# Sparse attention and a maxout layer on one core: a hand-set order up to the first maxout, v one batch ahead

## The chip, the cores and the metric

One core of one Trainium2 chip. The metric is the device time of one execution in microseconds (us), as a median over runs. The kernel before takes 225.36 us (three runs, 224.71 to 225.65). The profile's span is 1 to 2 us shorter than that time.

Engines are named as in the profile: PE multiplies matrices (PEld loads its weights), DVE and ACT work on vectors, POOL is the third vector engine, SP only issues DMAs. "PEq", "SPq", "POOLq" are the instruction queues of an engine.

## The reference, cut to what matters

```python
# q, k, v: [4 batches, 8 heads, 768 positions, 64], float32
k_sum = k.reshape(B, H, nb, 32, D).max(axis=3)      # 24 blocks per head
v_sum = v.reshape(B, H, nb, 32, D).mean(axis=3)
mask_l = np.abs(pos[:, None] - pos[None, :]) < 16   # a band
# softmax over [band scores, block scores + log 32], times [v, v_sum]
x = attention.transpose(0, 2, 1, 3).reshape(3072, 512)
out = np.maximum(x @ w1, x @ w2) @ w_out            # d_model 512, d_ff 1024
```

Both kernels rewrite the maxout as `x @ (w1 @ w_out) + relu(x @ (w2 - w1)) @ w_out`. The product `w1o = w1 @ w_out` is made once, on the chip, and so is a piece of work with no counterpart in the reference.

## The kernel before

Queries are cut into 12 tiles of 64. A tile needs the 96 positions of k around it and 24 block sums. The same 96 positions of v are gathered by copies from `vb` into `vext`. The block means of v go into `vext` too: a matmul makes them (`vs_ps`), a DVE copy writes tile 0, and one broadcast DMA fills the other 11 tiles. These are the parts that the change touches:

```python
def load_batch(b):                      # all on SP's queue, in this order
    for hp in range(NP):
        for src, tag in ((k, "kf"), (q, "qf"), (v, "vf")):
            loads[tag, b, hp] = load_pair(src, b, hp, tag)

def prep_v(b):
    vbt, vx = vb[b % 2], vext[b % 2]
    for hp in range(NP):
        nc.vector.tensor_copy(...)      # cast of v, four times      (cut)
    for j in range(2):
        r = j * 48
        nc.sync.dma_start(out=vx[r:r + 48, 0], in_=vbt[0:48, 0, j])
        nc.sync.dma_start(out=vx[r:r + 48, 1:NT:4], in_=vbt[24:72, :, j])
        # ... six more for each j: 16 copies in all                  (cut)
    ps = psum.tile([128, H, D], F32, tag="tr", bufs=2, name="vs_ps")
    # ... six matmuls of the means into ps                           (cut)
    nc.vector.tensor_copy(out=vx[96:NK, 0, :, 0:D], in_=ps[96:NK])
    nc.sync.dma_start(...)              # the broadcast              (cut)

load_batch(0)
prep_v(0)
load_weights()
for _ in attention(0):
    pass
cast_weights()
make_w1o()
for b in range(B):
    side = iter(())
    if b + 1 < B:
        load_batch(b + 1)
        prep_v(b + 1)
        side = attention(b + 1)
    for _ in maxout(b):                 # one step of each in turn
        next(side, None)
    for _ in side:
        pass
```

The softmax here doesn't subtract the row's maximum and nothing guards it: scores larger than these inputs give would overflow.

Of the kernel before, what the change touches and what calls it, by code (L numbers as in the profile page):

```python
# [12 lines left out]
F32 = mybir.dt.float32  # L13
# [7 lines left out]
def kernel(  # L21
# [23 lines left out]
    NK = 96 + nb  # L45
    VW = 66

    def g0(t):
        return 0 if t == 0 else (336 if t == NT - 1 else 32 * t - 8)
# [5 lines left out]


    identity = const.tile([128, 128], BF16, name="identity")
    make_identity(nc, identity[:])
# [3 lines left out]
    m0 = const.tile([128, 3, 64], F32, name="m0")  # L62
    m1 = const.tile([128, 3, 64], F32, name="m1")
    for m, j in ((m0, 0), (m1, 1)):
        nc.gpsimd.memset(m[:], 1.0)
        for w, off in enumerate((0, -16, -32)):
            base = off - 95 * j
            sl = m[:, w, :]
            nc.gpsimd.affine_select(out=sl, in_=sl, compare_op=ALU.is_ge, fill=0.0,
                                    base=base + window - 1, channel_multiplier=2,  # L70
                                    pattern=[[-1, 64]])
            nc.gpsimd.affine_select(out=sl, in_=sl, compare_op=ALU.is_ge, fill=0.0,
                                    base=window - 1 - base, channel_multiplier=-2,
                                    pattern=[[1, 64]])
    nc.gpsimd.affine_select(out=m0[:], in_=m0[:], compare_op=ALU.is_ge, fill=0.0,
                            base=47, channel_multiplier=-1, pattern=[[0, 3], [0, 64]])
    nc.gpsimd.affine_select(out=m1[:], in_=m1[:], compare_op=ALU.is_ge, fill=0.0,
                            base=-48, channel_multiplier=1, pattern=[[0, 3], [0, 64]])
    nc.gpsimd.tensor_tensor(out=m0[:], in0=m0[:], in1=m1[:], op=ALU.add)
    nc.gpsimd.memset(m0[96:128], 1.0)  # L80
    mask = const.tile([128, NT, 64], BF16, name="mask")
    nc.gpsimd.tensor_copy(out=mask[:, 0:2, :], in_=m0[:, 0:2, :])
    nc.gpsimd.tensor_copy(out=mask[:, NT - 2:NT, :], in_=m0[:, 1:3, :])
    nc.gpsimd.tensor_copy(out=mask[:, 2:NT - 2, :],
                          in_=m0[:, 1:2, :].to_broadcast([128, NT - 4, 64]))

    bias = const.tile([128, 1], F32, name="bias")
    nc.gpsimd.memset(bias[:], 0.0)
    nc.gpsimd.memset(bias[96:128], logblk)


    amean = const.tile([128, 3, 128], BF16, name="amean")
    nc.gpsimd.memset(amean[:], 1.0 / block)
    nc.gpsimd.affine_select(out=amean[:], in_=amean[:], compare_op=ALU.is_ge, fill=0.0,
                            base=96 * 16, channel_multiplier=1, pattern=[[128, 3], [-16, 128]])
    nc.gpsimd.affine_select(out=amean[:], in_=amean[:], compare_op=ALU.is_ge, fill=0.0,
                            base=15 - 96 * 16, channel_multiplier=-1,
                            pattern=[[-128, 3], [16, 128]])


    NBUF = 3
    kext = [const.tile([128, NT, 128], BF16, name=f"kext{i}") for i in range(NBUF)]
    qbd = [const.tile([128, NT, 128], BF16, name=f"qbd{i}") for i in range(NBUF)]
    NPB = 4
    prob = [const.tile([128, 8 * 128], BF16, name=f"prob{i}") for i in range(NPB)]
    vb = [const.tile([128, 3, 2, H, VW], BF16, name=f"vb{i}") for i in range(2)]
    vext = [const.tile([128, NT, H, VW], BF16, name=f"vext{i}") for i in range(2)]
    for i in range(NBUF):
        nc.gpsimd.memset(qbd[i][0:64, :, 64:128], 0.0)
        nc.gpsimd.memset(qbd[i][64:128, :, 0:64], 0.0)  # L110
        nc.gpsimd.memset(kext[i][:, :, NK:128], 0.0)
    for i in range(NPB):
        nc.vector.memset(prob[i][:], 0.0)
    for i in range(2):
        nc.gpsimd.memset(vb[i][:, :, :, :, D:VW], 1.0)
        nc.gpsimd.memset(vext[i][96:NK, :, :, D:VW], 1.0)

# [3 lines left out]
    w1b = const.tile([128, KC, d_ff], BF16, name="w1b")  # L121
    w1t = const.tile([128, FC, d_model], BF16, name="w1t")
# [14 lines left out]
    def load_batch(b):  # L137
        for hp in range(NP):
            for src, tag in ((k, "kf"), (q, "qf"), (v, "vf")):
                loads[tag, b, hp] = load_pair(src, b, hp, tag)  # L140
# [3 lines left out]
    def load_weights():  # L144
        w1v = moe_w1.rearrange("(kc p) n -> p kc n", p=128)
        w2v = moe_w2.rearrange("(kc p) n -> p kc n", p=128)
        wov = moe_w_out.rearrange("(fc p) n -> p fc n", p=128)
        for c in range(KC):
            w1f = stage.tile([128, d_ff], F32, tag="w1f", bufs=4, name="w1f")
            nc.sync.dma_start(out=w1f[:], in_=w1v[:, c, :])  # L150
            wof = stage.tile([128, 2, d_model], F32, tag="wof", bufs=2, name="wof")
            nc.sync.dma_start(out=wof[:], in_=wov[:, 2 * c:2 * c + 2, :])
            w2f = stage.tile([128, d_ff], F32, tag="w2f", bufs=2, name="w2f")
            nc.sync.dma_start(out=w2f[:], in_=w2v[:, c, :])
            wload[c] = (w1f, w2f, wof)

    def cast_weights():
        for c in range(KC):
            w1f, w2f, wof = wload[c]
            nc.vector.tensor_copy(out=w1b[:, c, :], in_=w1f[:])  # L160
            nc.vector.tensor_tensor(out=wd[:, c, :], in0=w2f[:], in1=w1f[:], op=ALU.subtract)  # L161
            nc.scalar.copy(out=wo[:, 2 * c:2 * c + 2, :], in_=wof[:])  # L162

    def make_w1o():
        for f in range(FC):
            ps = psum.tile([128, KC, 128], BF16, tag="tr", bufs=2, name="w1t_ps")
            for c in range(KC):
                nc.tensor.transpose(out=ps[:, c, :], in_=w1b[:, c, f * 128:f * 128 + 128],
                                    identity=identity[:])
            nc.vector.tensor_copy(out=w1t[:, f, :], in_=ps[:].rearrange("p c n -> p (c n)"))  # L170
        for c in range(KC):
            ps = psum.tile([128, d_model], F32, tag="o", bufs=1, name="w1o_ps")
            for f in range(FC):
                nc.tensor.matmul(out=ps[:], lhsT=w1t[:, f, c * 128:c * 128 + 128],  # L174
                                 rhs=wo[:, f, :], start=(f == 0), stop=(f == FC - 1))
            nc.vector.tensor_copy(out=w1o[:, c, :], in_=ps[:])


    def prep_v(b):
        vbt, vx = vb[b % 2], vext[b % 2]  # L180
        for hp in range(NP):
            nc.vector.tensor_copy(  # L182
                out=vbt[:, :, :, 2 * hp:2 * hp + 2, 0:D].rearrange("p c j h d -> p (c j) h d"),
                in_=by_slot(loads["vf", b, hp]))
        for j in range(2):
            r = j * 48

            nc.sync.dma_start(out=vx[r:r + 48, 0], in_=vbt[0:48, 0, j])
            nc.sync.dma_start(out=vx[r:r + 48, 1:NT:4], in_=vbt[24:72, :, j])
            nc.sync.dma_start(out=vx[r:r + 48, 2:NT:4], in_=vbt[56:104, :, j])  # L190
            nc.sync.dma_start(out=vx[r:r + 40, 3:8:4], in_=vbt[88:128, 0:2, j])
            nc.sync.dma_start(out=vx[r + 40:r + 48, 3:8:4], in_=vbt[0:8, 1:3, j])
            nc.sync.dma_start(out=vx[r:r + 8, 4:9:4], in_=vbt[120:128, 0:2, j])
            nc.sync.dma_start(out=vx[r + 8:r + 48, 4:9:4], in_=vbt[0:40, 1:3, j])
            nc.sync.dma_start(out=vx[r:r + 48, NT - 1], in_=vbt[80:128, 2, j])
        ps = psum.tile([128, H, D], F32, tag="tr", bufs=2, name="vs_ps")
        for c in range(3):
            for j in range(2):
                nc.tensor.matmul(out=ps[:], lhsT=amean[:, c, :], rhs=vbt[:, c, j, :, 0:D],  # L199
                                 start=(c == 0 and j == 0), stop=(c == 2 and j == 1))  # L200
        nc.vector.tensor_copy(out=vx[96:NK, 0, :, 0:D], in_=ps[96:NK])
        nc.sync.dma_start(
            out=vx[96:NK, 1:NT].rearrange("p t h w -> p t (h w)"),
            in_=vx[96:NK, 0:1].rearrange("p t h w -> p t (h w)").to_broadcast(
                [nb, NT - 1, H * VW]))

    def prep_kq(b, hp):
        i = (b * NP + hp) % NBUF
        kx, qx = kext[i], qbd[i]
# [3 lines left out]
        nc.vector.tensor_copy(out=qb[:], in_=by_slot(loads["qf", b, hp]))  # L213
# [185 lines left out]
```

## Time and profile before

| | before |
|---|---|
| time, median | 225.36 us |
| span of the profiled run | 224.2 us |
| PE busy | 174.6 us, 78% |
| DMA traffic | 37.68 MB |

Lines of the page of the kernel before. Each digit is the busy share, in tenths, of one of 40 equal slices of the span; PEclk is the granted clock of PE in tenths.

```profile
PE   0003832665788999896989999999999999999973
PEclk9999999997699999999999999999999999999999
DMA  6998438999997335999634599634431101202112
```

Three slices (17 us) pass before PE has anything to do, another eight before it is full; after that it is full to the end. The page shows one dip of the granted clock, at 50 to 62 us. The trace's record of the clock begins only at 43 us here, so the 9s before that are no measurement: the first six matmuls of 512 columns, at 20 us, came 0.43 us apart, twice the 0.215 us of later ones.

The table by stretches of the kernel before. The columns are the stretch and its length, the busy time of each engine with its count of instructions, the granted clock, the mean share of the DMA engines and what they moved.

```profile
0.00:20.00 20.00, 0.00 (x0) 0.10 (x1) 7.94 (x12) 1.28 (x1) 15.35 (x45) 1.00 1.01 270
20.00:40.00 20.00, 10.76 (x81) 7.56 (x81) 11.22 (x23) 8.12 (x11) 1.16 (x2) 1.00 0.55 162
40.00:63.00 23.00, 15.84 (x181) 11.59 (x182) 21.44 (x51) 11.27 (x16) 0.86 (x2) 0.85 1.04 326
63.00:80.00 17.00, 15.43 (x108) 8.24 (x108) 11.30 (x22) 5.88 (x11) 1.05 (x2) 1.00 0.66 173
80.00:100.00 20.00, 18.90 (x184) 11.61 (x186) 10.48 (x29) 11.58 (x21) 0.43 (x1) 1.00 0.78 202
100.00:120.00 20.00, 17.33 (x158) 10.33 (x158) 13.83 (x34) 10.97 (x19) 1.17 (x2) 1.00 0.70 194
120.00:200.00 80.00, 77.19 (x681) 45.46 (x692) 41.84 (x103) 46.13 (x82) 3.85 (x7) 1.00 0.40 114
```

Three lines of the view of waits for PE, before: who waited for what, us in total, how often, the longest.

```profile
PE vs_ps L199 <- DVE vb_113 L182: 20.4, 1, 20.4
PE av L277 <- DMA vext_115<-vext_115: 4.1, 1, 4.1
PE o_ps L339 <- ACT osb L347: 1.4, 2, 0.7
```

PE first waits 20.4 us for the cast of v, and later 4.1 us until the copies of v and the broadcast have landed. The head of the kernel is latency, most of it behind v. From 80 us on PE is the bound.

### The profile page before, as it was taken

Reading aid. Unit: us, or ns where it says so; the run is one execution under the profiler, and the core shown is the slowest. Engines: PE = TensorE matmul, PEld = TensorE weight load, DVE = VectorE, ACT = ScalarE, POOL = GpSimd, SP = SyncE. Lnnn points to the kernel's source line nnn. Section 1 sums busy time; section 2 is a strip of 40 time slices with the busy share of each in tenths; the row PEclk is TensorE's granted clock in tenths of the full one; section 3 lists DMA queues with packets and bytes.
Section 4 is the critical chain, followed back from the end, with each engine's and each line's share of the span. In section 5 each row is a group of like instructions: output and inputs, shape, how many; then the busy total and the mean of one; then the engine's idle time right before and its main releaser. Section 6 shows DMA issues by size and latency. Waiting matters only on the chain.

```text
span 224.2 us, 3831 instructions
## 1 busy us (share of the span) xinstructions
PE 174.6 (78%) x1475; PEld 103.8 (46%) x1496; DVE 118.0 (53%) x268; ACT 102.7 (46%) x173; POOL 23.9 (11%) x61
## 2 busy tenths in 40 slices
PE   0003832665788999896989999999999999999973
PEld 0001622543553655664555466655546664544531
DVE  5432852899972950896857069844727853000000
ACT  2000651575120573585179248824935972442521
POOL 8990110000000010000011001000000000000000
PEclk9999999997699999999999999999999999999999
DMA  6998438999997335999634599634431101202112
GB/s 187 289 290 273 106 100 251 375 365 283 288 281 183 90 90 135 288 292 282 184 117 102 158 259 306 163 116 152 103 87 50 51 0 47 96 0 95 47 47 94
DMA packets 49858, 37.68 MB, mean 168 GB/s; under 512 B 2192, under 2 KB 44720, under 8 KB 49840
## 3 DMA queue, kind: packets, MB, share of 16 engines
q1 hardware_dynamic: 49840, 37.45, 58.5%
q8 instruction: 11, 0.18, 0.3%
q14 instruction: 7, 0.06, 0.1%
HBM read 25.17 MB, written 6.29 MB: 140 GB/s over the span
## 4 chain that ended last, share of the span: by engine, by line
PE 49%; DMA 15%; DVE 13%; ACT 11%; SPq 7%; issue 3%; POOL 1%; ACTq 0%; POOLq 0%
PE o_ps L343 16%; DMA vf<-in_v_dram 13%; PE h_ps L330 11%; PE o_ps L339 8%; PE av L277 4%; PE sc L253 2%; ACT g L332 2%; PE x_ps L294 2%; DMA vext_115<-vext_115 2%; DVE wd L161 2%; SPq L127 2%; ACT qbd_107 L242 2%; PE vs_ps L199 2%; ACT qbd_108 L242 2%; PE w1o_ps L174 2%
## 5 line engine op out<-in xcount | busy, mean ns | idle before, releaser
L330 PE MATMUL h_ps<-xt,wd 128*128 128x384 bf16 x256 | 54.2, 331 | 2.5 <-DVE xt L296 1.1
L343 PE MATMUL o_ps<-wo,g 128*128 128x512 bf16 x186 | 46.5, 379 | 0.3
L332 ACT ACTIVATE g<-h_ps 128x384 bf16<-128x384 f32 x64 | 30.1, 491 | 15.7 <-PE h_ps L330 15.2
L347 ACT COPY osb<-o_ps 128x512 f32<-128x512 f32 x24 | 14.1, 586 | 49.2 <-PE o_ps L343 49.1
L330 PEld LDWEIGHTS <-wd 128*128 128x128 bf16 x256 | 23.7, 98 | 16.8 <-issue 3.0
L343 PEld LDWEIGHTS <-g 128*128 128x128 bf16 x192 | 17.9, 98 | 18.2
L339 PE MATMUL o_ps<-w1o,xt 128*128 128x512 bf16 x83 | 24.1, 378 | 2.1 <-ACT osb L347 1.4
L199 PE MATMUL vs_ps<-vb_113,amean 128*128 128x512 bf16 x12 | 4.2, 502 | 20.4 <-DVE vb_113 L182 20.4
L282 DVE RECIPROCAL inv<-av 128x6 f32<-128x6 f32 x32 | 6.1, 190 | 25.0 <-PE av L277 24.9
L284 DVE TENSOR_TENSOR x<-av,inv 128x384 bf16<-128x384 f32 x32 | 17.6, 550 | 0.3
L234 DVE TENSOR_REDUCE ks<-k_ps 128x24 bf16<-128x768 bf16 x16 | 15.1, 945 | 0.0
L162 ACT CAST wo<-wof 128x1024 bf16<-128x1024 f32 x4 | 4.2, 1043 | 23.8 <-DMA wof<-in_moe_w_out_dram 23.8
L339 PEld LDWEIGHTS <-xt 128*128 128x128 bf16 x96 | 9.1, 97 | 10.4 <-issue 4.0
L199 PEld LDWEIGHTS <-amean 128*128 128x128 bf16 x24 | 2.5, 107 | 24.3 <-issue 13.8
L296 DVE COPY xt<-x_ps 128x384 bf16<-128x384 bf16 x32 | 11.3, 352 | 2.8 <-PE x_ps L294 2.2
L294 PE MATMUL x_ps<-identity,x 128*128 128x128 bf16 x96 | 11.2, 230 | 1.4 <-ACT qbd_108 L242 0.6
L242 ACT COPY qbd_107<-q_ps 64x768 bf16<-64x768 bf16 x10 | 7.9, 792 | 9.3 <-PE q_ps L219 9.2
L255 ACT ACTIVATE prob_109<-sc,bias 120x512 bf16<-120x512 f32 x12 | 8.3, 689 | 7.8 <-PE av L277 6.7
L242 ACT COPY qbd_106<-q_ps 64x768 bf16<-64x768 bf16 x12 | 9.5, 793 | 4.0 <-PE q_ps L219 3.9
L213 DVE CAST qb<-qf 128x768 bf16<-128x768 f32 x16 | 10.3, 647 | 1.1 <-DMA qf<-in_q_dram 1.1
L182 DVE CAST vb_113<-vf 128x768 bf16<-128x768 f32 x8 | 5.1, 638 | 10.4 <-DMA vf<-in_v_dram 10.3
L219 PE MATMUL k_ps<-identity,kb 128*128 128x128 bf16 x96 | 9.8, 236 | 1.0 <-DVE ks L234 0.9
(94 smaller groups left out, 251.0 us busy)
## 6 DMA issues: line engine op xcount, KB each, us to landing
kf<-in_k_dram SPq DMA_DIRECT2D x16, 384.0 KB
qf<-in_q_dram SPq DMA_DIRECT2D x16, 384.0 KB
vf<-in_v_dram SPq DMA_DIRECT2D x16, 384.0 KB
out_dram<-osb SPq DMA_DIRECT2D x24, 256.0 KB
w1f<-in_moe_w_dram SPq DMA_DIRECT2D x4, 512.0 KB
wof<-in_moe_w_out_dram SPq DMA_DIRECT2D x4, 512.0 KB
w2f<-in_moe_w_dram SPq DMA_DIRECT2D x4, 512.0 KB
vext_115<-vb_113 SPq DMA_DIRECT2D x8, 148.5 KB
```

The source lines that it names most:

```text
L199: nc.tensor.matmul(out=ps[:], lhsT=amean[:, c, :], rhs=vbt[:, c, j, :, 0:D], start=(c == 0 and j == 0), stop=(c == 2 and j == 1))
L213: nc.vector.tensor_copy(out=qb[:], in_=by_slot(loads["qf", b, hp]))
L234: nc.vector.tensor_reduce(out=ks[:], in_=kps.rearrange("p j (n g) -> p n j g", g=16), axis=AX.XY, op=ALU.max)
L242: nc.scalar.copy(out=qx[r, :, a * 64:a * 64 + 64].rearrange("p t (g j) -> p t g j", j=2), in_=qps[r].rearrange("p j (t g) -> p t g j", g=32))
L284: nc.vector.tensor_tensor(out=x[:], in0=av[:, :, :, 0:D], in1=inv[:].to_broadcast([128, 3, 2, D]), op=ALU.mult)
L294: nc.tensor.transpose(out=ps[:, u, :], in_=xs[half][:, u].rearrange("p a d -> p (a d)"), identity=identity[:])
L296: nc.vector.tensor_copy(out=xts[b, half][:, hp, :], in_=ps[:].rearrange("p u n -> p (u n)"))
L330: nc.tensor.matmul(out=h[:], lhsT=wd[:, c, f * 128:f * 128 + 128], rhs=xt[:, c, :], start=(c == 0), stop=(c == KC - 1))
L332: nc.scalar.activation(out=g[:, f, :], in_=h[:], func=ACT.Relu)
L339: nc.tensor.matmul(out=ps[:], lhsT=xt[:, c, sl], rhs=w1o[:, c, :], start=(c == 0), stop=False)
L343: nc.tensor.matmul(out=ps[:], lhsT=g[:, f, sl], rhs=wo[:, f, :], start=False, stop=(f == FC - 1))
L347: nc.scalar.copy(out=o[:, u, :], in_=ps[:])
```

## The change

Its intent: scores do not need v, so let them go first; gather v with 6 copies, not 16, by cutting v into uniform chunks of 96 positions with a margin; start the maxout with half of d_ff as soon as half of the weights are in; and load, cast and copy v of each later batch one batch ahead, with the casts, copies and broadcasts issued from POOL. PE's and the other engines' order up to the end of the first maxout is fixed by hand; later batches are still ordered by the scheduler. PSUM buffers: `av` 2 in place of 1, `h` and `o` share 2. The core of the diff (cut where marked):

```diff
-    def load_batch(b):
-        for hp in range(NP):
-            for src, tag in ((k, "kf"), (q, "qf"), (v, "vf")):
-                loads[tag, b, hp] = load_pair(src, b, hp, tag)
+    def load_kq(b, hp):
+        for src, tag in ((k, "kf"), (q, "qf")):
+            loads[tag, b, hp] = load_pair(src, b, hp, tag)
+
+    def load_v(b):
+        src = v[b].rearrange("h (g j) d -> g h (j d)", j=2)
+        # ... six loads on SP's queue into vf[0..3], each vf one buffer (cut)
+    def cast_v(b, engines):
+        for u, e in engines:
+            (nc.vector if e == "v" else nc.gpsimd).tensor_copy(
+                out=vb[b % 2][:, u, :, :, 0:D], in_=vf[u].rearrange("p h (j d) -> p j h d", j=2))
+
+    def spread_v(b, queue):
         vbt, vx = vb[b % 2], vext[b % 2]
-        # ... four casts on DVE, 16 copies on SP                        (cut)
+        for w in range(3):
+            for j in range(2):
+                queue.dma_start(out=vx[j * 48:j * 48 + 48, w:NT:3],
+                                in_=vbt[32 * w:32 * w + 48, :, j])
+
+    def mean_v(b, queue):
+        # ... eight matmuls into vs_ps, the DVE copy                    (cut)
+        queue.dma_start(...)                # the broadcast             (cut)
-    load_batch(0)
-    prep_v(0)
-    load_weights()
-    for _ in attention(0):
-        pass
-    cast_weights()
-    make_w1o()
+    def first_attention():
+        for hp in range(2):                 # casts, transposes, scores
+            ...                             # of pairs 0 and 1          (cut)
+        cast_v(0, ((0, "v"), (1, "p"), (2, "p"), (3, "v")))
+        spread_v(0, nc.sync)
+        mean_v(0, nc.gpsimd)
+        load_weights()                      # in halves of d_ff
+        ...                                 # pairs 2, 3; values        (cut)
+    with tc.manual_schedule():
+        first_loads()
+        first_attention()
+        load_v(1)
+        for hp in range(NP):
+            load_kq(1, hp)
+        for _ in first_maxout():            # hidden half of batch 0, and
+            pass                            # the transposes of w1
+        cast_v(1, ((u, "p") for u in range(NU)))
+        spread_v(1, nc.gpsimd)
+
+        def second():
+            a = attention(1)
+            for _ in range(3):
+                next(a)
+                yield
+            mean_v(1, nc.gpsimd)
+            yield from a
+
+        def rest():
+            yield from make_w1o()
+            yield from output(0, 0)
+            yield from output(0, 1)
+
+        weave(rest(), second(), 1.3)
+    for b in range(1, B):
+        side = iter(())
+        if b + 1 < B:
+            load_v(b + 1)
+            for hp in range(NP):
+                load_kq(b + 1, hp)
+            cast_v(b + 1, ((u, "p") for u in range(NU)))
+            spread_v(b + 1, nc.gpsimd)
+            mean_v(b + 1, nc.gpsimd)
+            side = attention(b + 1)
+        weave(maxout(b), side, 1.0)
```

## The prediction

> **What bounds it now.** Two parts. Up to about 58 us, latency: the table by stretches gives PE 10.8 us busy in 20-40 and 10.4 in 40-57, nothing before 20. The view of waits shows 20.4 us of PE waiting for the last v cast, then 4.1 us for the copies of v: 16 issues at about 0.73 us each and a broadcast, 20.4 to 36.7 us. DVE is 15.9 of 17 us busy in 40-57, weight casts included (0.69 + 1.21 us, four times). From 58 us PE bounds: at 80-220.7 I count 133.5 us of matmul pace (0.162 us per 384 columns, 0.215 per 512, 0.056 per 128) in 140.7 us. So only some 7 us of stalls can be saved there, some of them output tiles waiting 0.67 us for their single PSUM buffer.
>
> **What the change does.**
> 1. Scores no longer wait behind v on PE: k, q of pair 0 are first on the queue. PE starts at about 5 us, not 20.4.
> 2. Copies of v 16 to 6 issues (0.65 us each, about 4 us), but they copy 2.4 MB, from about 21 us (after the masks of pair 1 on DVE). Landed at about 31 us.
> 3. Against this, the first attention becomes a serial chain of short steps: place k 2.1 us on DVE (0.65 + 0.25 + 0.95 + about 0.3 for the fill now on DVE), q 1.6 us on ACT, three exps 1.9, masks, then x and transposes. Adding these in order I get pair 1's masks at 19, the mean of v at 25, pair 3 placed at 34, first `av` at 34, first `h_ps` at about 48 us.
> 4. Splitting d_ff starts maxout after half of the weights; all 64 hidden matmuls and the w1 transposes are done at about 63 us (before: a quarter of them and of w1o).
> 5. PE work is almost unchanged (vs_ps 6 to 8 matmuls per batch: +0.43 us each). From 63 us about 141 us at pace remain. That is 7-8 us ahead of before.
> 6. v casts (about 1.1 us each, an estimate from POOL's 0.61 us for 512 elements) and v copies go to POOL, kext fills (0.5 us) to DVE. DVE is then about 29 us of 40 per batch: not the bound, except beside w1o, where its fixed order costs waits of PE: I allow 5-7 us, also for v of batch 1, whose load queues behind the output weights.
> 7. Two PSUM buffers for `av`, nine `prob`, two shared by `h` and `o`: saves about 3 us of stalls. The tail (3.5 us after the last matmul) is unchanged.
>
> The first attention runs slow on PE: the Trainium skill, "TensorE: Matmul & The Clock Gate", Part 1, has the default state throttled to half rate until some 3.4 us of activity. This trace agrees: the first six 512-column matmuls took 2.72 us, 0.43 apart, against 0.215 later. The new order's gaps will keep it slow until maxout, at little cost: DVE and ACT bound there.
>
> **Sum.** 63 + 141 + about 5 to 9 of stalls + 3.5 = about 213 to 216 us of span, plus 1.1 to the time; as my hand chain may be pessimistic: **213 us**, 205 to 220. Chances: faster by 2% 0.87, within 0.11, slower 0.02.
>
> **What would show it.** First `sc` near 9 us; `vext` landed near 31; first `h_ps` 44-50; PE over 90% busy from there except in the w1o stretch; `o_ps` waiting for `osb` near zero; maxout of batch 3 still 26 us.
>
> **What would make it wrong.** v of batch 1 (loads, POOL casts, POOL-issued copies) landing past 75 us stalls PE's fixed order and eats the gain, or a first attention finished by 40 us (then about 205).

## The result, and the profile after

The changed kernel takes 234.75 us (four runs: 232.63 and 233.29 fast, 236.21 and 237.41 slow); before, in the same rounds, 225.48 us (224.71 to 225.65). The ratio of fast runs is 1.034, interval 1.029 to 1.039: slower. A ratio here is the mean time of one kernel's fast runs over the mean of the other's fast runs of the same rounds, so it is not quite the ratio of the medians quoted. The prediction was 213 us.

| | before | after |
|---|---|---|
| span of the profiled run (both fast) | 224.2 us | 231.6 us |
| PE busy | 174.6 us | 183.7 us |
| DMA traffic | 37.68 MB | 38.48 MB |
| first `h_ps` matmul | 40.2 us | 47.0 us |
| all 64 hidden matmuls of batch 0 and the transposes of w1 done | 97.8 us (hidden) | 63.1 us |
| matmuls on v of batch 1: the first (its tile needs no broadcast) / the next | 79.5 / 89.1 us | 72.4 / 82.2 us |

The same lines of the page, after.

```profile
PE   1446378599975078874999899999989999999993
PEclk9999999999999569996799999999999999999999
DMA  6999979799999999999999935002301200202112
```

PE starts in the first slice and is full from the ninth. Then come holes (the digits 5 and 0 at 69 to 81 us, 7 and 4 at 98 to 110) that the kernel before does not have, each with a low clock in it and after it; and the DMA engines are busy from 6 to about 133 us with hardly a pause.

The table by stretches, after.

```profile
0.00:20.00 20.00, 6.86 (x50) 5.19 (x51) 11.74 (x33) 9.91 (x13) 11.50 (x46) 1.00 1.04 226
20.00:40.00 20.00, 13.50 (x122) 9.93 (x120) 10.49 (x25) 8.62 (x12) 8.97 (x13) 1.00 0.92 241
40.00:63.00 23.00, 19.67 (x155) 12.44 (x153) 11.57 (x24) 8.65 (x17) 8.70 (x10) 1.00 1.01 269
63.00:80.00 17.00, 7.92 (x60) 4.16 (x56) 9.20 (x19) 7.41 (x10) 3.61 (x6) 0.86 1.13 241
80.00:100.00 20.00, 15.24 (x143) 9.20 (x144) 13.45 (x30) 6.77 (x10) 9.93 (x12) 0.86 1.18 208
100.00:120.00 20.00, 16.22 (x131) 8.98 (x129) 9.31 (x22) 5.99 (x9) 4.96 (x7) 0.83 1.13 272
120.00:200.00 80.00, 76.70 (x720) 47.41 (x719) 47.28 (x118) 48.66 (x84) 2.02 (x3) 1.00 0.32 90
```

Up to 63 us PE was busy for 40.0 us (6.86 + 13.50 + 19.67) where it had been for 26.6: 13 us more. In the next 37 us it was busy for 23.2 where it had been for 34.3: 11 us given back, and more in effect, as busy time at a clock of 0.86 does less.

Lines of PE's waits, after.

```profile
PE av L319 <- DMA vext_102<-vext_102: 9.7, 1, 9.7
PE k_ps L253 <- DVE kb L239: 8.8, 3, 4.7
PE av L319 <- DVE prob_92 L305: 3.6, 1, 3.6
```

The first is the hole at 72 to 82 us: the second matmul on v of batch 1 waits for the broadcast of the means. The second is the start of the kernel (the first k arriving) and was expected. The third is part of the hole near 100 us.

The timeline around the first hole: start, duration, queue or engine, line, operation, tiles, and in brackets the idle time before it and what ended it.

```profile
60.94 1.04 POOL L212 CAST vb_100<-vf_81 112x1024 bf16<-112x1024 f32 x1 [0.73 <-DMA vf_81<-in_v_dram]
62.29 3.61 POOL L219 DMA_DIRECT2D vext_102<-vb_100  x6 [0.31 <-POOL vb_100 L212]
67.73 7.30 SPq L150 DMA_DIRECT2D vf_78<-in_v_dram  x2
68.83 1.03 PE L202 MATMUL w1o_ps<-wo,w1t 128*128 128x512 bf16 x4
69.69 1.89 PE L227 MATMUL vs_ps<-vb_100,amean 112*128 112x512 bf16 x8
72.61 0.71 POOL L230 DMA_DIRECT2D vext_102<-vext_102  x1 [6.71 <-DVE vext_102 L229]
74.18 0.24 DVE L278 COPY kext_86<-ks 128x288 bf16<-128x288 bf16 x1
82.24 0.54 PE L319 MATMUL av<-vext_102,prob_93 120*128 120x65 bf16 x7 [9.68 <-DMA vext_102<-vext_102]
83.00 1.49 PE L202 MATMUL w1o_ps<-wo,w1t 128*128 128x512 bf16 x3
83.97 0.42 DVE L305 TENSOR_TENSOR prob_95<-prob_95,mask 120x512 bf16<-120x512 bf16 x1 [9.55 <-ACT prob_95 L301]
```

The loads of v of batch 1 landed at 60.9 us. POOL's last cast ended at 62.0, its six copies were issued by 65.9, the means were begun at 69.7, and the broadcast (272 KB) was issued at 72.6. It landed at about 82.1 us: 9.5 us; the last of the six copies, ahead of it in POOL's queue, had landed at 75.7. Meanwhile, from 67.7 us, SP was issuing loads of v for batch 2. The delay does not need these loads: in run a below they are gone, in h SP issued only loads of k and q until 76.5 us, and the broadcast still took 8.2 and 9.3 us. The cold clock adds to the loss: three matmuls of 512 columns took 1.49 us after the hole, four took 1.03 before it. This agrees with the clock gate that the Trainium skill, "TensorE: Matmul & The Clock Gate", Part 1, describes.

The view of DMAs, after, gives packets by queue; q1 is what SP issues, q0 what POOL issues. First for 66 to 70 us, when the six copies are under way, then for 74 to 78 us, when the broadcast is. Columns: packets, MB, share of 16 engines' time.

```profile
q0 software_dynamic: 185, 0.59, 70.1%
q1 hardware_dynamic: 591, 0.30, 39.6%
```

```profile
q1 hardware_dynamic: 1964, 0.99, 113.4%
q0 software_dynamic: 20, 0.04, 4.6%
```

In the first window POOL's queue moved twice as much as SP's (0.59 MB to 0.30), in fewer and larger packets. In the second the broadcast had been issued for 1.4 us and more, and POOL's queue, the end of the copies included, moved 0.04 MB in 4 us while SP's loads moved 0.99.

The kernel before did not have v of batch 1 any sooner. Its broadcast was issued later than this one landed:

```profile
82.34 0.82 SPq L202 DMA_DIRECT2D vext_116<-vext_116  x1
```

It lost nothing by it, because its PE had hidden and output matmuls and scores to do between its first matmul on v, at 79.5 us, and the next, at 89.1. In the changed kernel's fixed order nothing else stood between the two. So "late" here means late for this order of PE.

The second hole, near 100 us, is one of DVE's order: the cast of q for pair 1 of batch 2 waited for its load, issued at 91.9 and landed at 106.1 us behind v, and the masks that PE needed stood behind that cast.

```profile
106.20 0.56 DVE L244 CAST qb<-qf 128x768 bf16<-128x768 f32 x1 [3.94 <-DMA qf<-in_q_dram]
```

### The profile page after: what moved, and what is told of

It is laid out like the page before. It is cut to its first block, busy times and chain, and to the rows that moved or that the text cites. A ratio compares the mean times of both kernels' runs of the same rounds, so it can differ in the third digit from the quotient of the medians.

```text
span 231.6 us, 3876 instructions
## 1 busy us (share of the span) xinstructions
PE 183.7 (79%) x1504; PEld 110.7 (48%) x1504; DVE 113.0 (49%) x269; ACT 108.0 (47%) x177; POOL 49.7 (21%) x95
## 2 busy tenths in 40 slices
DMA packets 48819, 38.48 MB, mean 166 GB/s; under 512 B 1953, under 2 KB 41505, under 8 KB 48801
## 4 chain that ended last, share of the span: by engine, by line
PE 59%; ACT 13%; DMA 12%; DVE 10%; issue 4%; SPq 0%; ACTq 0%; DVEq 0%
PE o_ps L399 16%; PE h_ps L383 15%; PE o_ps L395 8%; DMA qf<-in_q_dram 8%; PE sc L296 4%; DMA vext_102<-vext_102 4%; PE vs_ps L227 4%; PE av L319 3%; ACT qbd_87 L284 3%; PE x_ps L337 2%; ACT qbd_88 L284 2%; PE q_ps L253 2%; PE k_ps L253 2%; PE w1o_ps L202 2%; ACT g L385 2%
## 5 line engine op out<-in xcount | busy, mean ns | idle before, releaser
L383 PE MATMUL h_ps<-xt,wd 128*128 128x384 bf16 x256 | 51.2, 336 | 1.6 <-ACT g L385 1.0
L399 PE MATMUL o_ps<-wo,g 128*128 128x512 bf16 x192 | 48.3, 385 | 0.0
L403 ACT COPY osb<-o_ps 128x512 f32<-128x512 f32 x24 | 14.1, 585 | 39.5 <-PE o_ps L399 39.4
L395 PE MATMUL o_ps<-w1o,xt 128*128 128x512 bf16 x96 | 25.7, 389 | 0.6 <-DVE w1o L206 0.6
L253 PE MATMUL k_ps<-identity,kb 128*128 128x128 bf16 x96 | 9.3, 241 | 11.1 <-DVE kb L239 8.8
L253 PEld LDWEIGHTS <-kb 128*128 128x128 bf16 x96 | 7.4, 108 | 15.5 <-DVE kb L239 10.0
L230 POOL DMA_DIRECT2D vext_102<-vext_102 x2 | 1.4, 704 | 45.5 <-DVE vext_102 L229 45.5
L337 PEld LDWEIGHTS <-x 128*128 128x128 bf16 x96 | 7.4, 109 | 7.3 <-DVE x L327 4.4
L253 PE MATMUL q_ps<-identity,qb 128*128 128x128 bf16 x96 | 9.3, 242 | 1.7 <-ACT qb L242 1.7
L296 PE MATMUL sc<-qbd_87,kext_84 128*128 128x128 bf16 x72 | 7.7, 247 | 3.3 <-ACT qbd_87 L284 2.6
L202 PE MATMUL w1o_ps<-wo,w1t 128*128 128x512 bf16 x32 | 9.6, 415 | 0.6 <-ACT wo L182 0.5
L239 DVE CAST kb<-kf 128x768 bf16<-128x768 f32 x16 | 9.2, 574 | 1.6 <-DMA kf<-in_k_dram 1.5
```

The costliest lines, as they stand in the source:

```text
L202: nc.tensor.matmul(out=ps[:], lhsT=w1t[f // 4][:, f % 4, c * 128:c * 128 + 128], rhs=wo[:, f, :], start=(f == 0), stop=(f == FC - 1))
L253: nc.tensor.transpose(out=ps[:, j, c * 128:c * 128 + 128], in_=src[:, 2 * c + j].rearrange("p h d -> p (h d)"), identity=identity[:])
L296: nc.tensor.matmul(out=sc[:, i // 2, :, i % 2], lhsT=kx[:, t0 + i, :], rhs=qx[:, t0 + i, :].rearrange("p (a q) -> p a q", a=2), start=True ...
L337: nc.tensor.transpose(out=ps[:, u, :], in_=xs[half][:, u].rearrange("p a d -> p (a d)"), identity=identity[:])
L383: nc.tensor.matmul(out=h[:], lhsT=wd[:, c, f * 128:f * 128 + 128], rhs=xt[:, c, :], start=(c == 0), stop=(c == KC - 1))
L395: nc.tensor.matmul(out=ps[:], lhsT=xt[:, c, sl], rhs=w1o[:, c, :], start=(c == 0), stop=False)
```

## The experiments

Theories: **A**, v of the later batches comes late because of what stands in the DMA queues and in the jam of loads (its parts: the loads a batch ahead, POOL's queue, and the order of loads); **B**, the fixed order with its serial chains is at fault, and PE would idle with v in place too. Texts before the runs also write C for "POOL's queue is starved by the loads on SP" (in c, e, g and h) and V for "volume and order of the loads alone". Each run stands beside runs of the kernel before on the same chip; those had medians of 225.0 to 225.9 us. All outputs were right but where noted. Diffs are against the changed kernel unless another is named.

| kernel | median us | range | ratio of fast runs to before |
|---|---|---|---|
| after | 234.75 | 232.63–237.41 | 1.034 |
| a, no loads of v for batches 2, 3 (wrong) | 226.63 | 226.27–227.42 | 1.003 |
| b, no v traffic from batch 1 on (wrong) | 215.41 | 215.29–215.93 | 0.955 |
| c, copies and broadcasts on SP | 224.94 | 221.1–227.06 | none |
| d, all of w1o first | 234.1 | 231.09–237.09 | 1.024 |
| e, c with the mean early | 227.06 | 225.26–227.73 | 1.007 |
| f, e with k, q before v in later batches | 228.39 | 227.9–232.21 | 1.013 |
| g, f with the copies before pairs 2, 3 | 227.26 | 223.93–229.24 | none |
| h, k, q before v in later batches, POOL's queue | 233.93 | 232.59–234.89 | 1.036 |
| i, all v traffic of batch 1 before pairs 2, 3 | 222.01 | 221.56–227.14 | 0.984 |
| j, scores of three pairs first | 224.0 | 223.8–224.11 | 0.992 |
| k, before, without v traffic from batch 1 on (wrong) | 223.74 | 222.82–225.14 | 0.990 |
| m, i with POOL's queue again | 234.38 | 231.3–236.27 | 1.029 |
| l, j with its chain pipelined | 219.71 | 219.26–222.81 | 0.973 |
| n, l with the casts of q on ACT | 216.84 | 216.79–217.45 | 0.962 |

"None" means that the fast runs did not give a ratio with an interval: the runs of c and g spread over 5 to 6 us.

### a: no loads of v for batches 2 and 3 (wrong result)

```diff
     def load_v(b):
+        if b >= 2:
+            return
```

> Wrong on purpose for batches 2 and 3 (they reuse the v of batch 1). Theory A (the DMA engines are saturated from 20 to 125 us, and the v loads of batches 2 and 3, 3.7 MB pulled ahead, delay what batch 1 and the start of batch 2 need): the broadcast of batch 1's mean lands before 78 us instead of 82.1, the q of batch 2, pair 1, no longer holds DVE for 3.9 us, PE's wait for vext_102 falls from 9.7 us to below 5; time 223 to 228 us. Rival B (PE's fixed order beside w1o is at fault, whatever the data do): PE loses the same 20 us and the time stays at 231 to 236 us.

226.63 us. The time is as expected, but not in the way expected: the broadcast, issued at 74.6 us, landed at 82.9, not before 78, and PE still waits 8.4 us for `vext` (it goes on at 83.0 us). What is gone is the second hole: 19.04 of 20 us busy in 100 to 120, against 16.22.

```profile
PE av L321 <- DMA vext<-vext: 8.4, 1, 8.4
```

```profile
100.00:120.00 20.00, 19.04 (x172) 11.29 (x174) 11.90 (x30) 9.00 (x15) 4.21 (x7) 1.00 0.88 231
```

The loads of v of batches 2 and 3 cost 0.031 of 225 us, 7 us, mostly in the second hole. The run takes the loads away altogether, so it does not price their being early alone.

### b: no loads, copies or broadcast of v from batch 1 on (wrong result)

```diff
     def load_v(b):
+        if b >= 1:
+            return
     def spread_v(b, queue):
+        if b >= 1:
+            return
     def mean_v(b, queue):
         # ... matmuls and the DVE copy stay (cut)
+        if b >= 1:
+            return
         queue.dma_start(...)
     def values(b, hp, grp):
-        vx = vext[b % 2]
+        vx = vext[0]
```

> Wrong on purpose for batches 1 to 3: no v load, no copies and no broadcast after batch 0; the casts, the mean's matmuls and all other work stay. Theory A: PE's waits between 63 and 120 us shrink to some 5 us, PE stays at full clock, and the time is 212 to 217 us, what I predicted for the change. Rival B (fixed order): still over 226 us.

215.41 us. The table by stretches of b, for 63 to 80 and 80 to 100 us:

```profile
63.00:80.00 17.00, 14.43 (x132) 8.54 (x133) 14.01 (x31) 10.65 (x14) 3.99 (x4) 1.00 0.33 94
80.00:100.00 20.00, 17.92 (x187) 10.90 (x190) 15.88 (x41) 10.12 (x15) 0.00 (x0) 1.00 0.74 212
```

The same fixed order now keeps PE 14.43 of 17 us busy (7.92 before) at full clock, with the DMA engines at 0.33. Theory B falls as it was put: with v in place PE does not idle. The fixed order keeps a part in it, though, since it is this order that asks for v at 72.4 us with nothing else to do. From a to b the ratio falls by another 0.049, 11 us. b also drops the copies and broadcasts of batches 2 and 3, but the two runs part before those are used: the maxout of batch 1 begins at 116.4 us in a and at 105.3 in b, 11.1 us apart, and at the end they are 12.0 apart. So nearly all of it is v of batch 1, and PE's wait for it in a is 8.4 us of it.

### c: copies and broadcasts on SP's queue

```diff
-        spread_v(1, nc.gpsimd)
+        spread_v(1, nc.sync)
-            mean_v(1, nc.gpsimd)
+            mean_v(1, nc.sync)
-            spread_v(b + 1, nc.gpsimd)
-            mean_v(b + 1, nc.gpsimd)
+            spread_v(b + 1, nc.sync)
+            mean_v(b + 1, nc.sync)
```

> The copies and broadcasts of v from batch 1 on are issued from SP, behind the loads, instead of from POOL. If the whole volume is what counts (theory A), the last v data of batch 1 land at about 80 us as now, and the time stays within 228 to 235 us. If it is POOL's queue that is starved by the loads (theory C: between 74 and 78 us it moved 20 of 1985 packets), the broadcast lands at about 75 us, PE's wait falls from 9.7 to about 3 us and the time to 223 to 227 us.

224.94 us, 10 us under the changed kernel by medians, with a correct result. The four runs spread from 221.1 to 227.06, three of them counted as slow, so there is no ratio. The wait for `vext` shrinks to 6.0 us. By medians, in which slow runs count on both sides, all that the change lost comes back with this edit; the one fast run, 221.1 us, is 12 us under the changed kernel's fast runs. The spread is not explained, and a better test of the queue is m, below.

### d: w1o as a whole before anything of batch 1

```diff
+        for _ in make_w1o():
+            pass
         def rest():
-            yield from make_w1o()
```

> All of w1o (6.9 us of PE) runs before attention of batch 1 instead of between its steps. Theory A: the data arrive when they arrive, but PE fills some 5 us of the wait for them, and the time falls to 227 to 230 us. Rival B: PE meets the same latencies later, no change, 231 to 236 us.

234.1 us: a miss. PE is 14.33 of 17 us busy in 63 to 80, and then 5.58 of 20 in 80 to 100. The mean of v and its broadcast stand behind w1o too, so the wait only moved, and grew to 14.1 us. More work in front of a late transfer is no help when the transfer is itself released by a later step of the same engine.

### e: SP's queue, and the mean of v as the first step of batch 1

```diff
         def second():
             a = attention(1)
-            for _ in range(3):
-                next(a)
-                yield
-            mean_v(1, nc.gpsimd)
+            mean_v(1, nc.sync)
+            yield
             yield from a
```

with `nc.sync` everywhere, as in c.

> Copies from SP as in the run before, and the mean of batch 1's v is taken at the start of the w1o stretch, so that the broadcast follows the copies at once. Theory C (what is late is the v data of batch 1, and on SP it goes in the order of issue): the broadcast is issued at about 70 us instead of 73.3, lands at about 76 instead of 79.8, PE's wait falls from 6.0 to about 3 us, and the time to 219 to 222 us. If the loads' volume alone set the arrival, it lands at 79 to 80 us again and the time stays at 221 to 225.

227.06 us: a miss. PE goes on at 81.5 us. The copies were issued at 68.4 to 75.3 us, because on SP's queue they now stood behind the k and q load of pair 3, which waited for its staging buffer. The broadcast followed at 75.3.

### f: e, and k, q before v in the loads of later batches

```diff
-            load_v(b + 1)
             for hp in range(NP):
                 load_kq(b + 1, hp)
+            load_v(b + 1)
```

> As the run with the early mean, and from batch 2 on the k and q loads are queued ahead of the v loads. If it is v being a batch ahead that costs (theory A), this gains another 2 to 4 us, 216 to 219 us, with DVE no longer waiting for a q of batch 2. If with the copies on SP the loads of batch 2 are early enough anyway, it is the same within 1 us.

228.39 us: a miss, 0.006 more than e. The two waits for `vext` are 5.5 and 4.4 us. What comes after v of batch 1 in the queue is not what delays it on SP's queue.

### g: f, and the copies before the loads of pairs 2 and 3

```diff
         load_v(1)
-        for hp in range(NP):
+        for hp in range(2):
             load_kq(1, hp)
...
+        spread_v(1, nc.sync)
+        for hp in range(2, NP):
+            load_kq(1, hp)
```

> As the run with k and q first, and the copies of batch 1's v stand in SP's queue before the k and q loads of its pairs 2 and 3. Theory C: the last v data land at about 73 us, when PE asks for them, PE's wait for them is below 1.5 us; time 213 to 217 us, near the 215.4 us of the run without v traffic. If it is the volume, the wait moves to the k of pair 2 (DVE waits over 3 us for it), and the time stays at 218 to 222 us.

227.26 us, from 223.93 to 229.24. PE goes on at 81.3 us: now the broadcast, issued at 73.0, stood behind the loads of pairs 2 and 3. In c, e and g the last of `vext` landed at 79.8 to 81.5 us although the order differed: each time some load was in front of one of its two transfers.

### h: only the order of loads, POOL's queue kept

The diff is that of f alone.

> The changed kernel with only the order of the loads from batch 2 on turned round: k and q ahead of v; the copies stay on POOL's queue. Theory A (v a batch ahead is the main cost): 224 to 228 us. Theory C (POOL's queue starved by the loads on SP, whichever they are): PE's wait for the broadcast of batch 1 stays at 7 to 10 us and the time at 228 to 233 us.

233.93 us, as the changed kernel. As a test of theory A it is not clean: the scheduler still hoisted loads of v of batch 3 in front of others. It says that this edit does nothing by itself. For the first hole it says more: until 76.5 us SP issued loads of k and q only, and the broadcast, issued at 72.0 us, still took 9.3 us and PE's wait 9.5.

### i: all v traffic of batch 1 before the loads of pairs 2 and 3, on SP's queue

The other copies and broadcasts go to `nc.sync` too, as in c (cut).

```diff
         load_v(1)
-        for hp in range(NP):
+        for hp in range(2):
             load_kq(1, hp)
...
         def second():
             a = attention(1)
-            for _ in range(3):
-                next(a)
-                yield
-            mean_v(1, nc.gpsimd)
+            mean_v(1, nc.sync)
+            for hp in range(2, NP):
+                load_kq(1, hp)
+            yield
             yield from a
```

> As the run with the copies before pair 2, but the broadcast too stands ahead of the k and q loads of pairs 2 and 3 of batch 1. Theory V (the DMA engines deliver at a fixed rate and all of batch 1's data were in by about 81 us in every order so far; what an order can do is to put first what is asked first): v is whole at about 75 us, PE's wait at the first values falls from 7.8 to below 2.5 us, and the k of pair 2 comes in time; time 218 to 222 us. If the wait only moves to the k of pair 2 and PE stalls for it by 4 us or more, 224 to 228 us.

222.01 us, ratio 0.984, interval 0.977 to 0.991: all three fast runs lie under all runs of before, but whether by 2% is unclear. The queue of SP in i (timeline), and PE's wait for v:

```profile
62.69 5.17 SPq L219 DMA_DIRECT2D vext<-vb  x6
67.95 1.07 SPq L230 DMA_DIRECT2D vext<-vext  x1
69.06 1.19 SPq L132 DMA_DIRECT2D kf<-in_k_dram  x1
```

```profile
PE av L319 <- DMA vext<-vext: 1.4, 1, 1.4
```

The wait went from 9.7 to 1.4 us, and PE goes on at 76.0 us. What is left is short waits for `kb`, `qbd`, `prob` and `x` beside w1o.

### j: scores of three pairs before the first values

Loads of three pairs come before the copies, and all copies and broadcasts go to `nc.sync` (cut).

```diff
         def second():
-            ...                      # attention(1), step by step (cut)
+            mean_v(1, nc.sync)
+            load_kq(1, 3)
+            for hp in range(3):
+                prep(hp)             # cast, transpose, place
+                yield
+                for grp in range(3):
+                    scores(1, hp, grp)
+                    yield
+            ...                      # then the values, pair by pair (cut)
```

> Copies on SP, mean first, loads in the order k and q of pairs 0 to 2, copies, broadcast, pair 3; and beside w1o PE does the scores of three pairs of batch 1 before any values, as the first attention does, so that it asks for v some 8 us later. Theory V: no PE wait for v over 1.5 us, PE over 85% busy from 63 to 100 us, and the time is 214 to 219 us, below both kernels. If DVE, which then has 16 us of work in a row beside w1o, is the next bound: 219 to 224 us with PE waiting for place steps.

224.0 us, ratio 0.992. PE waits for v no more, but `kb` (14.1 us in seven waits, where the changed kernel has 8.8 in three, at its start) and `qbd` (9.2 in nine) take its place: each pair is cast, transposed and placed right before its scores, a chain through DVE, PE, DVE and ACT with nothing between.

### k: the kernel before without v traffic from batch 1 on (control, wrong result)

```diff
             for src, tag in ((k, "kf"), (q, "qf"), (v, "vf")):
-                loads[tag, b, hp] = load_pair(src, b, hp, tag)
+                if tag == "vf" and b >= 1:
+                    loads[tag, b, hp] = loads[tag, 0, 3]
+                else:
+                    loads[tag, b, hp] = load_pair(src, b, hp, tag)
-        for j in range(2):
+        for j in range(2 if b == 0 else 0):
...                                   # no broadcast either          (cut)
```

> A control, wrong on purpose: the kernel before without the v loads, copies and broadcasts of batches 1 to 3 (casts, means and all else stay). If its v traffic cost the kernel before little, as I read its few PE waits, it takes 220 to 225 us, and then the 215.4 us of the changed kernel without v traffic shows that the new head start is real and worth 5 to 9 us. If it falls to 213 to 217 us too, the head start is worth nothing and v traffic is a cost of both.

223.74 us, ratio 0.990. So v traffic of the later batches costs the kernel before 1%, and the changed one 8% (1.034 against 0.955). Without it on both sides the change is worth 0.990 - 0.955 = 0.035 of 225 us, 8 us. The head start was predicted as 7 to 8, but these 8 us also hold what the PSUM buffers saved and what the stalls beside w1o cost, so they fit it and do not measure it.

### m: i, with the copies and broadcasts back on POOL's queue

```diff
-        spread_v(1, nc.sync)
+        spread_v(1, nc.gpsimd)
-            mean_v(1, nc.sync)
+            mean_v(1, nc.gpsimd)
-            spread_v(b + 1, nc.sync)
-            mean_v(b + 1, nc.sync)
+            spread_v(b + 1, nc.gpsimd)
+            mean_v(b + 1, nc.gpsimd)
```

against i.

> The run with v ahead of pair 2 with one thing turned back: copies and broadcasts from batch 1 on go on POOL's queue again, everything else as there (222.0 us). If the queue itself matters, because what waits on POOL's queue is passed over by the loads on SP, PE's wait for v of batch 1 rises from 1.4 us to 6 to 10 us and the time to 228 to 234 us. If only the order in time of the issues matters, the time stays at 220 to 225 us.

234.38 us, fast runs 231.3 and 232.61, ratio 1.029 against 0.984 of i: 0.045 of 225, 10 us, for this edit. It turns back the queue alone, but SP's loads move in time with it, as lines of the timeline of m show:

```profile
62.03 1.29 SPq L132 DMA_DIRECT2D kf<-in_k_dram  x1
67.71 0.71 POOL L230 DMA_DIRECT2D vext<-vext  x1 [0.88 <-DVE vext L229]
```

SP, which no longer had the copies in its queue, issued k and q of pair 2 from 62.0 us, where i issued them after the broadcast, from 69.1, and v of batch 2 from 72.1, not 76.1. So with the queue i's order is lost too, and the 10 us are for both. No run keeps POOL's queue and holds SP's loads back. Its profiled run (236.27 us) is one of the slow ones, so only PE's waits and the order and landing of transfers are read from it, no sum of time. Two of PE's waits in m:

```profile
PE av L319 <- DVE prob L305: 10.2, 4, 9.3
PE av L319 <- DMA vext<-vext: 5.3, 1, 5.3
```

The wait of 5.3 us is a little under the 6 to 10 expected. The broadcast was issued at 67.7 us, as early as in i (67.95), and landed at 79.8: 12.1 us, where PE in i could go on 8.1 us after the issue. The last of the six copies ahead of it had landed only at 78.0. Against the changed kernel the broadcast was issued 4.9 us sooner and landed only 2.3 us sooner. The 9.3 us are a second hole, at 101 to 110 us: PE needs a mask, which DVE does after a cast of k, and that load of k, issued at 92.1 us behind three loads of v, landed only at 107.2. The load of k that i issued at 72.5 us took 7.4 us. In m the copies for the next batch were under way at the same time on POOL's queue; which of the transfers delayed which is not settled.

### l: j with its chain pipelined

```diff
             for hp in range(3):
-                prep(hp)
+                cast_kq(1, hp + 1, "v")
+                scores(1, hp, 0)
                 yield
+                if hp < 2:
+                    transpose_kq(1, hp + 1)
+                    place_kq(1, hp + 1)
+                    yield
...                                   # values interleaved likewise (cut)
```

against j (whose SP order it keeps).

> As the run with the scores first (224.0 us, no wait for v, but PE waits of 1.4 to 1.8 us for each pair's k cast and 0.9 us for each q placement), with the casts and transposes of the next pair moved ahead of the scores of this one. If those short waits are what is left of the loss, PE's waits for kb and qbd from 63 to 95 us fall from some 9 us to below 3 us and the time to 216 to 219 us. If DVE's sum of work is the bound there, the waits move to the masks and x, and it stays at 221 to 224 us.

219.71 us, ratio 0.973. The next pair's casts, transposes and placing now run while this pair's scores do: from 63 to 95 us PE's waits for `kb` and `qbd` are 2.5 us, where j has 8.0.

### n: l with the casts of q on ACT in batch 1

```diff
-            cast_kq(1, 0, "v")
+            cast_kq(1, 0, "a")
-                cast_kq(1, hp + 1, "v")
+                cast_kq(1, hp + 1, "a")
```

against l.

> As the pipelined run, and in batch 1 the q casts (0.55 us each on DVE) are on ACT (0.83 us each). If DVE is the bound beside w1o, 1 to 2 us faster than the pipelined run; if the chain through ACT (placement of q, exps) is, 0.5 to 2 us slower.

216.84 us (216.79 to 217.45), ratio 0.962, interval 0.958 to 0.967: the best of all correct kernels, 3.8% under before and 7% under the changed kernel (0.962 / 1.034). The table by stretches of n:

```profile
63.00:80.00 17.00, 13.40 (x106) 7.19 (x105) 12.26 (x26) 13.14 (x18) 0.00 (x0) 1.00 1.08 236
80.00:100.00 20.00, 18.65 (x204) 11.12 (x203) 14.84 (x38) 8.63 (x13) 4.42 (x4) 1.00 1.09 263
100.00:120.00 20.00, 18.69 (x162) 11.11 (x161) 11.76 (x28) 11.23 (x20) 2.08 (x2) 1.00 0.71 163
```

The DMA engines are nearly as full as in the changed kernel in 63 to 100 us (1.08 and 1.09 against 1.13 and 1.18), and PE is at 13.40 and 18.65 us at full clock. A full DMA side was not the trouble in itself; what landed late in it was. Part of the gain is that PE asks later here: its first matmul on v of batch 1 is at 82.2 us.

## Why the prediction was wrong

What it had right:

- **The head start.** First `sc` at 8.8 us (predicted near 9), first `av` at 32.7 with no wait for `vext` (landed near 31), first `h_ps` at 47.0 (44 to 50), the hidden half and the transposes done at 63.1 (63). From 48 to 63 us PE is 14.36 of 15 us busy. The controls (b against k) give the whole change without v traffic 8 us; 7 to 8 were predicted for the head start.
- **Small terms.** POOL's cast of v took 1.04 us (about 1.1). `o_ps` waits for `osb` no more (1.4 us before). The hidden and output matmuls of batch 3 begin at 200.7 us and end about 27 us later (26). The kext fills on DVE took 0.24 to 0.27 us, half of the 0.5 predicted.

What failed is one term, in step 6 and in the sum. The prediction put it: "except beside w1o, where its fixed order costs waits of PE: I allow 5-7 us, also for v of batch 1, whose load queues behind the output weights", and in the sum "about 5 to 9 of stalls". From 63.1 us to the end of the span at 231.6 are 168.5 us. Taking off its own 141 at pace and 3.5 of tail leaves 24 us of stalls and cold clock. So the term is off by 15 to 19 us. The fast runs average 233, 20 us over the prediction; the small rest is that the prediction took the low end of its own sum.

Where the 24 us went, by the runs:

1. **v of batch 1 comes 10 us after PE asks: 11 us** (b against a). Not the load: it landed at 60.9 us. Late were the steps after it: casts on POOL to 62.0, six copies, the mean only at 69.7, the broadcast at 72.6, 9.5 us until it landed. An earlier mean alone does not mend it (m). The prediction's last paragraph named it ("landing past 75 us") but gave slower only 0.02: step 6 names only the load, and no term of the sum prices the casts, copies and broadcast behind it. The broadcast of batch 0 had taken 6.9 us in this kernel.
2. **The loads of v a batch ahead: 7 us** (a against the changed kernel): they fill the DMA engines beside everything else and delay q of batch 2, in whose wait DVE's order holds back the masks. a takes these loads away and not only their earliness, but all v traffic of the later batches cost the kernel before only 2 us (k). No word of the prediction counts this.
3. **The rest, 6 us of 24**, is what 5 to 9 was meant for: b, with no v traffic after batch 0, still stands 2.4 us over 213.

The cause under 1 and 2 is in large part **which queue issues the copies**, and with it what SP loads ahead of and beside them: 10 us between m and i, whose programs differ in nothing else, and 10 by medians between the changed kernel and c. The prediction gave "POOL-issued copies" no cost of their own. The costs of queue and of loads overlap, so these 10 us are not to be added to the 7 and 11.

How the queue does it is only partly settled. The Trainium skill, "DMA: Bandwidth & Descriptors", section "SWDGE vs HWDGE vs iDMA", says that the two kinds of queue feed different internal queues of a DMA engine, between which it "round-robins". The trace shows a share that swings: in 66 to 70 us POOL's queue moved 0.59 MB to SP's 0.30, in 74 to 78 us it had 20 packets to 1964. That does not refute taking turns, as no view shows on which engines both queues had work. The Trainium skill, "SBUF — State Buffer", section "SBUF: two separate sides", offers another reason in its box on DVE blocking a DMA: POOL can't write descriptors while certain DVE operations run. For this broadcast it doesn't fit: the timeline above has DVE idle from 74.4 to 84.0 us, and the broadcast landed only at 82.1. And by the Trainium skill, "Perfetto Trace Analysis", section "DMA Instruction — SWDGE (GPSIMD)", the end of such an instruction in a profile is the end of writing descriptors: that was at 73.3 us here. If so, it was the DMA engines that passed the queue over while SP's had work. No run shows that directly, and i and m do not part it from the plain order of SP's loads. For the six copies the DVE's part stays open.

Also open: why c, g and m spread by 5 us and more from run to run; and what the order of loads of batch 3 costs alone, as h did not change it. How much of the 24 us is cold clock can be bounded: after 63 us the granted clock was 0.50 from 75.2 to 85.5 us and from 106.0 to 112.8, and PE was busy for 3.3 and 5.5 us of these. At half the pace that is an estimate of at most 4.4 us, inside terms 1 and 2.

## What to carry to other kernels

When a change gives one stage a head start, the next stage needs its data earlier by as much: trace every transfer that it waits for back to its issue, each with its queue, and with what is in front of it and what else is on the DMA engines at that time; here v of batch 1 was asked for at 72.4 us, 7 us sooner than before, with nothing else in PE's order to do meanwhile, and came at 82.2. Issue what the critical engine will wait for on the same queue as the bulk loads, ahead of them, and not on POOL's queue beside them. If a result can be made wrong, a run without the suspected traffic prices it in one go, and the same cut in the kernel before shows what the rest of the change is worth. After an edit of a queue, look in the trace at what else moved with it.

## What the Trainium skill lacked or had wrong

- "DMA: Bandwidth & Descriptors", section "SWDGE vs HWDGE vs iDMA": the round-robin between the two kinds of queue. It has no measured share. In the changed kernel POOL's queue moved 0.59 MB (185 packets) to SP's 0.30 (591) in 66 to 70 us, and 0.04 (20) to 0.99 (1964) in 74 to 78 us; the choice of queue, with the order of loads that goes with it, was worth 10 us of the kernel's time (m against i).
- "Trainium Kernel Development and Optimization", section "Key Constraints": that DMAs of SP, ACT and POOL run on the same engines and that issuing from several "only saves the sequencer's issue time". It lacks that the choice can cost: here moving the same transfers from SP to POOL, which also let SP's later loads go ahead of them, cost 10 us, although issuing the six copies took POOL less time (3.53 us in m) than SP (5.17 us in i).
- "DMA: Bandwidth & Descriptors", section "Anatomy of one DMA — SWDGE (gpsimd) path": its fit, 2.0 us plus bytes over 436e3, gives an estimate of 2.6 us for the broadcast of 272 KB. It took 9.5 us in the changed kernel and 12.1 in m, in each case with copies still ahead of it in its queue (until 75.7 and 78.0 us). The page has no figure for how long a transfer takes beside a full DMA side; the fit is of no use there.
- "SBUF — State Buffer", section "SBUF: two separate sides": the reason that its box gives for a slow DMA of POOL's queue is a busy DVE. The broadcast was slow with DVE idle for 9.55 us.
